# A long convolution and MLP on one core: the second half's two spectral products summed on VectorE before one step back, in a new hand-written order

## The chip, the cores and the metric

The kernel runs on one core of one Trainium2 chip. The metric is the device time of one execution in microseconds; the time before is the median of three runs. A profiled execution of the same program gives the trace; its span, from the first to the last instruction, is a little shorter than its device time.

The core has five engines with queues of their own, which run in the order in which instructions stand in them: TensorE (PE in the profile; its weight loads are listed as PEld), VectorE (DVE), ScalarE (ACT), GpSimd (POOL) and SyncE (SP, which here only starts DMA transfers). An instruction that waits holds up all that stands behind it in its queue.

## The reference

With S = 2048 rows, D = 512 channels and F = 1792:

```
kv = shift_conv4(k, shift_k) * v                                  # [S, D], four taps along S
y  = irfft(rfft(pad(kv)) * rfft(pad(ssm_k)))[:S] + kv * ssm_D     # causal convolution over S, per channel
h  = x + layernorm(x) * y                                         # x = A_q
n  = layernorm(h)
g  = gelu(layernorm(n) @ w1);  g shifted along S by -1, +1, -2, +2 rows in four channel groups;  x1 = n + g @ w2
out = h + x1 + gelu(layernorm(x1) @ w3) @ w4                      # bf16 in and out
```

The convolution is the part that the change touches: its product is made between two spectra, channel by channel.

## The kernel before

**Halves.** The sequence is cut into two interleaved halves of eight row blocks each. Tasks carry the half as `s` (0 or 1). A signal named A0 or A1 is the gated input kv of a half, F0 or F1 a half of the filter. The circular convolution of the whole becomes small ones: half 0 of the output needs the product A0 x F0, half 1 needs A0 x F1 + A1 x F0.

**Transforms as matmuls.** Each signal goes forward in two steps of small matmuls against tables of sines that are built at the start: `S1` (line 389), copied out of PSUM by `E1`, exchanged between partitions by eight DMAs `X` (L405), then `S2` (L413), copied out by `E2`. For F1 the copy also adds and subtracts the spectrum of F0 (a fold, L425, VectorE). E1, E2 and EV below all go through one helper, so that their copies stand at L257 in the profile, on ScalarE or VectorE as the order says.

**Product and step back.** `conv(s, prods)` (L465 to L496) works in four passes `kl`. In each, for every pair of spectra, VectorE makes two products of 128 x 2048 bf16 elements (tasks `P`, L474): one with the filter spectrum as it lies (x = 0) and one with its real and imaginary planes exchanged (x = 1). Each product goes to two of the eight buffers of `r_p`. After each, TensorE takes a step back `I2` (L484) of 16 matmuls of 32 x 64 weights, which accumulates in the same four PSUM banks. The first half has one pair, so two products and two steps per pass; the second half has two pairs, so four products and four steps. `EV` copies the four banks out, `XI` (L495) exchanges partitions by DMA, and `I1` (L502) is the last transform, after which VectorE forms `H` (L616): h with its row sum.

**The MLP around it.** For each pair of row blocks of a half: statistics of h, a normalised copy `hb` (L655 on GpSimd or VectorE, L653 on ScalarE), its transposes (by TensorE and a copy, or by DMA through DRAM), `W` (L699) and its gelu `U`, the mixing over rows `X2` (L722), its residual sum `S` (L725, VectorE) with a row statistic `SS`, a second normalised copy `lb`, transposes again (`LX`, with the copy `EX`), `M` (L777), seven steps of eight matmuls per pair, with gelus `G` (L781, ScalarE), and `O` (L790) per block, 14 matmuls against w4. `R` (L729) and `Z` (L792) are VectorE's last sums for a block, and `OUT` stores it. The MLP of the first half lies between the passes of the second half's convolution. `Q` (L506) are the row statistics of the query input, per block, and `QV`, `QP`, `QN`, `Y` make its normalised form; `dg` (L299 on GpSimd, L307 on VectorE) builds the diagonal matrices of the four taps, which the shift (`K`, L442) uses as weights; `KV` (L450) is the gating.

**What sets the order.** Tasks are declared with `add(name, engines, function, ...)`. The order in which their instructions are issued is written out in the string `ORDER` at the head of the file: each word is a task's number, the engine that takes it (P, V, A, G or S) and the PSUM banks or buffers that it takes. So the string fixes each engine's queue, the engine of each task that has a choice, and the place of every DMA on SP's queue. The numbers in braces in `add` are the costs and `port` a mark with which the string was once planned; they do nothing in the program. The waits between engines follow from the data and buffers that instructions share.

Of the kernel before, what the change touches and what calls it, by code (L numbers as in the profile page):

```python
# [9 lines left out]
P = 128  # L10
S = 2048
D = 512
# [3 lines left out]
NB = 8  # L16
XW = 258
KW = NB * 129 + 8

BF16 = mybir.dt.bfloat16  # L20
F32 = mybir.dt.float32
# [10 lines left out]
004S 029P0 000S 002S 003S 005S 008S 031V 037V 001S 030P 063P23 006S 055P45 009S 057P67 064V 007S 056A 038G 065P01 010S 058A 019S 059P45 033V 045G  # L32
061P23 060A 087P60 039G 036V 062A 095P71 046V 042V 066A 093P4 032G 043V 047A 074S 101P5 044A 034G 015S 094V 051P23 022S 088V 053P01 035G 023S 052A
040V 072S 089P4 024S 054A 049G 091P6 021S 090V 073S 041A 097P2 096V 050G 070S 092V 099P3 048A 069S 102V 068S 107P01 098V 109P67 017S 100V 108A 103P45
067S 110V 111P23 018S 104A 115P01 071S 113P67 112A 323V 105P45 324V 116A 211P20 106V 114A 117P01 212V 119S 118A 084P4567 326V 085A 081P2301 123S 329V
086V 120S 083A 215P4 020S 082A 330V 124S 078P0167 327V 125S 217P5 080A 216V 121S 079A 075P2367 012S 218V 011S 325V 076A 127P4501 016S 319V 328V 122S
077A 219P21 129V 126S 331G 128A 013S 220V 130P6701 139V01 132A 141V23 131A 133P4501 332G 134A 140P23670 147V45 142P 135A 333G 149V67 143A 337G0
148P45011 155V01 150P 343G1 144A 145S 221P2 340G2 157V23 152A 146S 334G3 014S 151A 136P6701 222V 137V 138A 156P23452 153S 158P 154S 163V45 225P0 159A
223P1 160A 165V67 161S 164P67230 162S 226V 166P 224V 175P45 167A 168V 213P0 176A 169S 183P67 214V 170S 185P23 184A 187P45 315S 186V 177P01 188A 189P67
178V 179P23 190A 181P45 180V 171P67 028S 182A 172P01 338V 192S 231P45 196S 335V 339A 349G0 173P23 316S 344V 336A 346G3 193S 341V 235P67 232A 355G1  # L40
195S 347V 174P10 236A 352G2 191S 350V 237P45 198S 358G 342A 356V 202P6723 197S 348A 353V 194S 345A 359G 204V 239P01 238A 371G 203V 241P23 240A 227P45
242A 229P01 372G 360V 228V 230A 199P6723 247S 361G0 373V 233P45 351A 364G1 200V 362P00 234A 374G2 365P1 384V 366A 377G3 208P6745 245S 363V 354A 375P11
243S 201V 385G 367P0 376A 244S 357A 378P1 386V 246S 369P2 379A 390V0 318S 209V 397G 387A1 382P3 248S 370A 250S 388P12 210V 368A 398G 391P6 249S 380P7
383A 389A 027S 392V 399G 251P2345 263V01 381A 393P0 253A 026S 400G3 265V23 395P1 025S 252A 317S 403V2 205P6745 396A 267V45 401P23 394A 404P3 502P1
402A 206V 405A 506P0 503V 408P2 507V 504A 406P3 269V67 508A 409A 264P67011 558V 407A 266P 207V 268P 559G 270P 560G 498P2 271A 272V 561G1 510P3 564G0
499V 274S 494P4 501V 273S 562P50 511V 565P6 514P7 563A 495V 566A 411V 254P0123 496A 567P50 515V 256A 275V01 569P4 568A 577P6 277V23 570A 257P2345 578A
412V 573P7 259A 255V 571P6 258A 279V45 579P4 572A 574A 281V67 575P5 580A 516A 276P01232 414V 500A 278P 513V 280P 576A 615G 512V 282P 581P6 505V 283A
616G 517V 284A 617G 413V 621G3 287V01 618A2 619P71 587G 622P4 582V 260P0123 620V 583S 584P5 623V 588G 262A 289V23 589G 291V45 591A1 590G0 293V67
624P40 593S 261V 636P6 592S 625A 634P7 416V 509V 288P23010 635A 594S2 290P 299V01 292P 285S 294P 301V23 628P4 296A 632P7 303V45 629A 298S 637A 626P0
286S 633A 305V67 630P1 295A 410V 627A 297S 300P67231 417V 631A 302P 415V 304P 306P 418V 641P4 307A 419G 308A 309S 310S 420V 421V0 427G3 638P0 424G1  # L50
430V2 585V 642V 497V 311P16 639V 312P72 640S 422V 643S 313P35 425V 423A 433G0 428V 314P40 426A 431V 439A3 595P10 445G 442V1 432A 603P2 436V2 429A 437V
597P6 596A 434V 446G 605P7 598A 438A 447V 599P1 448V2 435A 451G3 322V 458V 607P5 600A 470V 459G 449P33 452P6 601P1 450V 453A 471G 460V 604A 440V 454P6
602A 472G 441V 461A2 456P3 443V 474G1 462A3 444V 473G0 608A 476S 606A 612P2 482V 475S 457A 463S 483G 464S 609P1 484V 477S0 485A1 486G0 455A 487S 321V
488S 465S1 518P0 522P3 489S2 480P4 523V 478P5 519V 524A 468P3 520A 481A 466P7 644V 521V 645G 490P6 467A 525V 646G 469A 492P0 610V 320G 479A 647V2
534P3 491A 648V3 649S 493A 650S 542P4 535V 554P5 537V 536A 538P3 651S3 555V 546P7 543V 556A 586S 545V 526P1 544A 611S 539V 530P6 547V 540A 550P3 527V
# [38 lines left out]
def body(ctx, tc, fx, kt, q, v, sd, w1, w2, w3, w4, out):  # L94
# [200 lines left out]
    def dg(c):  # L295
        def f(e, sl):
            if e == GP:
                tap = r_k[:, c * KW + NB * 129:(c + 1) * KW].rearrange("p (j x) -> p j x", x=2)[:, :, 1:2]
                pool.affine_select(out=diag[:, c], in_=tap.to_broadcast([P, 4, P]), compare_op=OP.is_equal, fill=0.0, base=0,  # L299
                                   pattern=[[0, 4], [-1, P]], channel_multiplier=1)  # L300
                return
# [542 lines left out]
```

## Time and profile before

| | us |
|---|---|
| runs | 215.84, 214.04, 215.55 |
| median | 215.55 |
| profiled execution | 213.26 |
| its span | 211.6 |

The granted TensorE clock was 1.000 in the profiled execution. Its busiest groups on TensorE are the MLP's `M` and `O`; on VectorE the products, 24 in all; on ScalarE the copies out of PSUM and the gelus. DMA moved 32.86 MB, most of it in the first 80 us.

How to read the lines that follow: in the table of groups a line has the source line, engine, operation, what it writes and reads, the shape and count, then total busy us and the mean ns of one, then the engine's idle time just before them and what ended it. In a timeline a line has start, length, engine, source line, operation, count, and in brackets the idle time before it and its releaser. The chain of waits follows the work that ended last back from the end. In the slices, each digit is the busy share in tenths of a fortieth of the span.

### The profile page before, as it was taken

What the parts mean: (1) busy time and instruction counts of PE and PEld (TensorE: products, weight loads), DVE (VectorE), ACT (ScalarE), POOL (GpSimd) and SP (SyncE); (2) the same over time, 40 slices, a digit from 0 to 9 for tenths busy, and PEclk for the clock granted to TensorE, in tenths of its full rate; (3) what the DMA queues carried; (4) which work ended last, traced back from release to release, by engine and by line L of the source; (5) the groups of instructions that cost most, each with busy time, mean ns of one, the idle gap of its engine ahead of it and who ended that gap; (6) DMA issues with size and microseconds to landing.
All of it is one profiled execution on the core that took longest, in us unless ns stands there. A gap on an engine that the chain in (4) does not pass through costs nothing.

```text
span 211.6 us, 5040 instructions
## 1 busy us (share of the span) xinstructions
PE 195.7 (93%) x1964; PEld 116.2 (55%) x1980; DVE 144.8 (68%) x302; ACT 125.5 (59%) x206; POOL 80.1 (38%) x177
## 2 busy tenths in 40 slices
PE   6899769898889999979999999989999999999992
PEld 5454323442248546636744884645848888645450
DVE  6998999999999999999868971559972000112031
ACT  3979989787999658943751883364623565301010
POOL 7850059804888140287044683212765000000000
PEclk9999999999999999999999999999999999999999
DMA  6999895976948995000693008533146440010011
GB/s 173 313 403 397 321 325 222 256 205 237 371 169 294 332 435 147 0 28 13 89 232 92 27 22 181 98 69 82 42 107 154 102 74 0 3 50 34 16 50 50
DMA packets 30809, 32.86 MB, mean 155 GB/s; under 512 B 20545, under 2 KB 22594, under 8 KB 30530
## 3 DMA queue, kind: packets, MB, share of 16 engines
q1 hardware_dynamic: 30786, 32.55, 50.8%
q8 instruction: 15, 0.25, 0.5%
q14 instruction: 8, 0.07, 0.1%
HBM read 13.14 MB, written 4.46 MB: 83 GB/s over the span
## 4 chain that ended last, share of the span: by engine, by line
PE 59%; DVE 13%; ACT 12%; DMA 6%; issue 3%; POOL 3%; SPq 3%; DVEq 0%; ACTq 0%; POOLq 0%
PE ps L777 21%; PE ps L790 18%; ACT r_a L257 5%; PE ps L722 5%; PE ps L699 5%; PE ps L484 3%; DVE r_v L616 3%; DMA r_dg<-dhb 2%; DMA r_a<-r_a 2%; PE ps L502 2%; PE ps L413 2%; DMA r_k<-in_kt_dram 2%; DVE r_f L425 2%; DVE r_dg L307 1%; DVE r_p L474 1%
## 5 line engine op out<-in xcount | busy, mean ns | idle before, releaser
L777 PEld LDWEIGHTS <-r_k 128*128 128x128 bf16 x448 | 43.5, 98 | 7.7 <-issue 1.2
L792 DVE TENSOR_TENSOR r_v<-ps,r_v 128x512 bf16<-128x512 f32 x16 | 10.7, 686 | 42.4 <-PE ps L790 42.4
L474 DVE TENSOR_TENSOR r_p<-r_a,r_f 128x2048 bf16<-128x2048 bf16 x24 | 28.7, 1240 | 1.0 <-PE ps L484 0.6
L777 PE MATMUL ps<-r_dg,r_k 128*128 128x256 bf16 x224 | 25.6, 273 | 0.1
L257 ACT CAST r_a<-ps 128x1024 bf16<-128x1024 f32 x23 | 22.2, 1026 | 3.0 <-PE ps L413 2.8
L781 ACT ACTIVATE r_f<-ps 128x512 bf16<-128x512 f32 x14 | 7.8, 599 | 20.6 <-PE ps L777 20.6
L613 POOL TENSOR_SCALAR z_t<-r_q,qrs,qnm 128x512 f32<-128x512 bf16 x11 | 13.0, 1188 | 12.6 <-DVE r_v L616 12.0
L442 PE MATMUL ps<-r_dg,r_k 128*128 128x256 bf16 (+3 forms) x108 | 15.2, 284 | 1.6 <-ACT r_f L257 0.8
L257 ACT CAST r_vs<-ps 128x1024 bf16<-128x1024 f32 x14 | 13.7, 1032 | 4.9 <-PE ps L484 4.9
L725 DVE SCALAR_TENSOR_TENSOR r_q<-r_v,hrr,ps 128x512 bf16<-128x512 bf16 x16 | 11.4, 742 | 5.9 <-PE ps L722 3.7
L781 ACT ACTIVATE r_a<-ps 128x512 bf16<-128x512 f32 x14 | 7.8, 606 | 12.2 <-PE ps L777 12.2
L257 ACT CAST r_f<-ps 128x1024 bf16<-128x1024 f32 x14 | 13.2, 1023 | 3.0 <-PE ps L389 2.8
L442 PEld LDWEIGHTS <-r_k 128*128 128x128 bf16 x112 | 9.5, 98 | 9.5 <-issue 4.8
L484 PE MATMUL ps<-r_p,ttab 32*64 32x512 bf16 x384 | 13.3, 379 | 1.0 <-DVE r_p L474 0.8
L699 PEld LDWEIGHTS <-r_fx 128*128 128x128 bf16 x128 | 12.3, 98 | 3.2 <-DMA r_dg<-dhb 0.6
L600 ACT ACTIVATE junk<-r_v 128x512 bf16<-128x512 bf16 x14 | 8.9, 635 | 7.3 <-DVE r_v L616 7.1
L777 PE MATMUL ps<-xtx,r_k 128*128 128x256 bf16 x112 | 13.0, 273 | 0.0
L600 ACT ACTIVATE junk<-r_q 128x512 bf16<-128x512 bf16 x12 | 7.6, 630 | 9.2 <-DVE r_q L725 9.1
L777 PE MATMUL ps<-xty,r_k 128*128 128x256 bf16 x112 | 12.7, 272 | 0.0
L790 PE MATMUL ps<-w4s,r_f 128*128 128x512 bf16 x54 | 12.5, 379 | 0.1
L748 POOL TENSOR_TENSOR xrr<-xrr,mhalf 128x2 f32<-128x2 f32 x8 | 7.2, 900 | 14.2 <-DVE xrr L745 13.8
L389 PEld LDWEIGHTS <-f 128*32 128x32 bf16 x256 | 6.1, 95 | 11.3 <-issue 7.5
(183 smaller groups left out, 374.7 us busy)
## 6 DMA issues: line engine op xcount, KB each, us to landing
r_z<-r_vs SPq DMA_DIRECT2D x16, 256.0 KB, 3.9
r_k<-in_kt_dram SPq DMA_DIRECT2D x8, 260.0 KB, 4.6
r_v<-in_v_dram SPq DMA_DIRECT2D x4, 512.0 KB, 7.3
r_f<-r_f SPq DMA_DIRECT2D x8, 256.0 KB, 5.2
r_q<-in_q_dram SPq DMA_DIRECT2D x8, 256.0 KB, 5.7
r_a<-r_a SPq DMA_DIRECT2D x8, 256.0 KB, 4.2
r_f<-r_a SPq DMA_DIRECT2D x8, 256.0 KB, 4.2
r_a<-r_z SPq DMA_DIRECT2D x8, 256.0 KB, 4.1
```

The lines of the kernel that those rows point to most:

```text
L257: (act.copy if e in "AM" else on[e].tensor_copy)(o, i)
L442: nc.tensor.matmul(o[:, (d + j0) * P:(d + j1 + 1) * P], lhsT=kT[s][c][:, bb, x:x + P], rhs=diag[:, c, j0:j1 + 1, :].rearrange("p j x -> p ...
L474: on[e].tensor_tensor(out=prs[:, sl[0]:sl[0] + 2, :, :], in0=sp[a][:, kl, :, :, :], in1=gv, op=MUL)
L484: nc.tensor.matmul(ps[64 * t:64 * t + 64, bk[h], :], lhsT=ttab[32 * h:32 * h + 32, 2 * kl + t, 2 if x else xx, :], rhs=prs[32 * h:32 * h + ...
L600: act.activation(junk[:], x, ACT.Square, accum_out=sq[:, i, 1:2])
L613: on[e].tensor_scalar(out=z_t[:, sl[0], :], in0=qs, scalar1=qrs[:, i:i + 1], scalar2=qnm[:, i:i + 1], op0=MUL, op1=ADD)
L699: nc.tensor.matmul(ps[:, sl[0], j * 256:(j + 1) * 256], lhsT=w1s[:, k, m * P:(m + 1) * P], rhs=xt[:, k, :], start=(k == 0), stop=(k == DC ...
L725: vec.scalar_tensor_tensor(out=q_sb[:, s, b, :], in0=h_sb[s][:, b, :], scalar=hrr[:, 4 * s + b // 2, 0, b % 2:b % 2 + 1], in1=ps[:, got((" ...
L777: nc.tensor.matmul(ps[:, sl[0], j * 256:(j + 1) * 256], lhsT=w3s[:, k, fc * P:(fc + 1) * P], rhs=xt[:, k, :], start=(k == 0), stop=(k == D ...
L781: act.activation(gb[:, 2 * fp:2 * fp + 2, :], ps[:, got(("M", s, p, fp))[0], :].rearrange("p (j x) -> p j x", j=2), ACT.Gelu_apprx_tanh)
L790: nc.tensor.matmul(ps[:, sl[0], :], lhsT=gb[:, fc, (b % 2) * P:(b % 2 + 1) * P], rhs=w4s[:, fc, :], start=(fc == 0), stop=(fc == FC - 1))
L792: add(("Z", s, b), {V: 0.61}, lambda e, sl, b=b: vec.tensor_tensor(out=h_sb[s][:, b, :], in0=ps[:, got(("O", s, b))[0], :], in1=h_sb[s][:, ...
```

## The change

**The sum of products.** In `conv`, if there is more than one pair (the second half), VectorE adds the second pair's product to the first's in place (`PA`), and the step back is made on the sum alone: two steps `I2` per pass in both halves. The steps' weights don't depend on the pair, so the sum is the same but for a rounding to bf16. The second product's buffers come free with the addition. The rule that each product must follow the one declared before it is dropped.

```
-                    before = last_p[-1:]
...
-                    add(("P", s, kl, i, x), {V: 1.15}, f, [("E2", y, kl, t) for y in (a, g) for t in range(2)] + ["f2"] + before, take=[("pr", -1)], port="VG")
-                    last_p.append(("P", s, kl, i, x))
-                    first, last = (i, x) == (0, 0), (i, x) == (len(prods) - 1, 1)
...
+                    add(("P", s, kl, i, x), {V: 1.15}, f, [("E2", y, kl, t) for y in (a, g) for t in range(2)] + ["f2", "tt"], take=[("pr", -1)], port="VG")
+                    first, last, y = x == 0, x == 1, ("P", s, kl, 0, x)
+                    if i < len(prods) - 1:
+                        continue
+                    if i:
+                        def f(e, sl, x=x, kl=kl):
+                            pa, pb = (prs[:, got(("P", s, kl, j, x))[0]:got(("P", s, kl, j, x))[0] + 2, :, :] for j in range(2))
+                            vec.tensor_tensor(out=pa, in0=pa, in1=pb, op=ADD)
+                        add(("PA", s, kl, x), {V: 1.135}, f, [y, ("P", s, kl, i, x)], drop=[(("P", s, kl, i, x), 0)], port="VG")
+                        y = ("PA", s, kl, x)
```

**Row statistics of the query input.** For blocks 4 to 7 of the second half they are made by ScalarE, as a sum and a sum of squares, in place of one pass on VectorE; the variance step takes three more short instructions for them.

```
+        if s == 0 or b < 4:
+            return lambda e, sl: vec.bn_stats(qst[:, 8 * s + b, :], q_sb[:, s, b, :])
+
+        def f(e, sl):
+            act.activation(junk[:], q_sb[:, s, b, :], ACT.Identity, accum_out=qst[:, 8 * s + b, 0:1])
+            act.activation(junk[:], q_sb[:, s, b, :], ACT.Square, accum_out=qst[:, 8 * s + b, 1:2])
+        return f
```

**Diagonals.** `dg` can be made by GpSimd only; before, VectorE made two of the four (four instructions each) and GpSimd two.

**The order.** `ORDER` is a new string throughout: places in all queues, the engine of many tasks that have a choice, and banks. What the steps of the prediction speak of:

- VectorE, up to its last spectral pass: besides the eight additions it takes the first half's `QV` and `QN`, two `Y` and some short passes; it gives up both `dg`, five `Q` of the second half (four to ScalarE; those of blocks 1 to 3 now follow, and that of block 0 does as before), four `R` (they follow later), and on balance three copies out of PSUM (`E1`, `EV`) to ScalarE. The `EX` copies of blocks 2 and 3 are VectorE's now, those of blocks 0 and 1 ScalarE's.
- ScalarE: the four `Q`, the copies `E2` of A1 in pass 1 and 3, `EV` of passes that VectorE copied in part.
- GpSimd: four `dg`; `dr` and `f2v` (table and input preparation at the start) go to VectorE.
- TensorE: one `M` step of the first half's pair 2 stands ahead of the last pass `I2`; the second half's `I1` steps are interleaved with `M` steps; the first `M` of the second half's pair 1 precede `O` of blocks 6 and 7 of the first half.
- SP: `Lw3` and `Lw4`, the loads of w3 and w4 of 1.8 MB each, precede more of the second half's exchanges `X`; some input loads come later.

More of the change, by code (lines that the diff above doesn't have):

```diff
@@ L36 @@
[L36 to L39, printed above, removed]
@@ L296, in f @@
         def f(e, sl):
[L297 to L301, printed above, removed]
[L302 to L307 removed]
+            tap = r_k[:, c * KW + NB * 129:(c + 1) * KW].rearrange("p (j x) -> p j x", x=2)[:, :, 1:2]
+            pool.affine_select(out=diag[:, c], in_=tap.to_broadcast([P, 4, P]), compare_op=OP.is_equal, fill=0.0, base=0,
+                               pattern=[[0, 4], [-1, P]], channel_multiplier=1)
         return f
     for c in range(DC):
[L310 removed]
+        add(("dg", c), {GP: 0.65}, dg(c), [("Lk", 0, c)], port="VG")
     sv = small("sv", 8, F32)
@@ L461, in kvsrc @@
         return lambda b: kvs[:, got(("K", 2 * s + b // 4, 0), "kv")[0], b % 4, :]
-    last_p = []
     def conv(s, prods):
```

85 lines of the change are left out of this document (43 added, 42 removed).

## The prediction

> **What bounds the kernel now.** I read the page first (engine totals, the span in slices), then the windows over the stages that it suggests, then the chain of waits and single engines' timelines where stages meet.
>
> ```profile
> span 211.6 us, 5040 instructions
> ...
> PE 195.7 (93%) x1964; PEld 116.2 (55%) x1980; DVE 144.8 (68%) x302; ACT 125.5 (59%) x206; POOL 80.1 (38%) x177
> ...
> DVE  6998999999999999999868971559972000112031
> ```
>
> TensorE is busy for 93% of the span, but VectorE's row of slices holds nines almost to the middle and little in the last quarter. The kernel has two regimes, and the windows separate them (after the length: PE, PEld, DVE, ACT, POOL, then the granted clock, 1.00 throughout):
>
> ```profile
> 49.60:69.20 19.60, 18.00 (x225) 8.98 (x226) 19.18 (x48) 18.39 (x35) 16.16 (x32) 1.00 0.74 269
> 69.20:109.70 40.50, 38.91 (x529) 23.61 (x519) 37.95 (x62) 26.94 (x45) 13.97 (x24) 1.00 0.52 154
> ...
> 113.90:207.90 94.00, 92.71 (x626) 61.06 (x632) 38.63 (x107) 39.28 (x81) 23.54 (x44) 1.00 0.28 65
> ```
>
> From 113.9 on TensorE has work for 92.7 of 94.0 us and the others for two fifths: there the end is TensorE's alone. From 49.6 to 109.7 TensorE and VectorE are both nearly full; in the second stretch only ScalarE has room, 40.50 - 26.94 = 13.6 us. The chain of waits shows how the regimes meet:
>
> ```profile
> 102.26 3.60 PE ps L777 x32
> 105.86 1.87 PE ps L484 x64
> 107.73 0.16 issue
> 107.89 5.99 PE ps L790 x27
> 113.88 0.04 issue
> 113.92 3.61 PE ps L502 x16
> ...
> 207.82 0.69 DVE r_v L792
> ```
>
> The last pass of the second half's step back (L484, 64 matmuls) ends at 107.73, two output blocks of the MLP (L790) fill 6.0 us, and the second half's last transform (L502) starts at 113.92. In those 6 us the result is copied out by ScalarE and carried over by DMA:
>
> ```profile
> 101.04 4.63 DVE L474 TENSOR_TENSOR r_p<-r_a,r_f 128x2048 bf16<-128x2048 bf16 x4 [0.63 <-PE ps L484]
> 105.58 1.87 DVE L506 BATCH_NORM_STATS2 qst<-r_q 128x6 f32<-128x512 bf16 x3
> ...
> 107.78 1.93 ACT L257 CAST r_vs<-ps 128x1024 bf16<-128x1024 f32 x2 [1.03 <-PE ps L484]
> ```
>
> VectorE's last product ends at 105.6, just as TensorE reaches that pass; ScalarE's copies end at 109.7; the transform starts 4.2 later and TensorE has hardly idled. Three engines arrive level.
>
> **What the change costs, part by part.**
>
> *Matmuls taken away.* Each of the second half's four passes loses two of its four steps. A pass takes 1.87, a step so 0.47, and 8 steps are 3.7 us of TensorE, all ahead of 107.7. It is a gain only if TensorE then doesn't wait for what feeds the transform.
>
> *Additions put on VectorE, and what leaves it.*
>
> ```profile
> L474 DVE TENSOR_TENSOR r_p<-r_a,r_f 128x2048 bf16<-128x2048 bf16 x24 | 28.7, 1240 | 1.0 <-PE ps L484 0.6
> L729 DVE SCALAR_TENSOR_TENSOR r_v<-r_q,hnm,r_v 128x512 bf16<-128x512 bf16 x16 | 11.5, 740 | 0.1
> ...
> L257 DVE CAST r_a<-ps 128x1024 bf16<-128x1024 f32 x9 | 10.8, 1214 | 0.4 <-PE ps L389 0.3
> ...
> L425 DVE TENSOR_TENSOR r_f<-ps,r_f 128x512 bf16<-128x512 f32 x16 | 10.1, 679 | 0.0
> L307 DVE TENSOR_SCALAR r_dg<-ident,r_k 128x128 bf16<-128x128 bf16 x8 | 3.1, 466 | 0.5 <-DMA r_k<-in_kt_dram 0.5
> ...
> L613 DVE TENSOR_SCALAR z_t<-r_q,qrs,qnm 128x512 f32<-128x512 bf16 x4 | 2.0, 541 | 0.0
> ...
> L655 DVE TENSOR_SCALAR nbx<-r_q,xrr,xnm 128x512 bf16<-128x512 bf16 x3 | 1.1, 407 | 0.0
> ```
>
> No row shows an addition. The nearest is the product, which moves the same three tiles: 4.63/4 = 1.16 apiece in a run, 1.24 on the mean. Four block scalings (0.41 each) move as many elements and take longer, so no row gives a lower bound under 1.16. I take 1.16: eight are 9.3 us (up to 9.9).
>
> Comparing the two queues up to VectorE's last spectral pass: five row statistics leave (1.87/3 = 0.62 apart, 3.1), four residual sums move behind (0.74, 3.0), three copies out of PSUM go to ScalarE on balance (1.21, 3.6), both diagonal builds go to GpSimd (3.1): 12.8 off. On come the 9.3, two query passes (0.54, 1.1), the first half's variance in nine steps of a few elements, which I estimate at a third of a block scaling each (1.2), and on balance two short passes (0.41, 0.8): 12.4. Net -0.4: the additions are paid for.
>
> Two waits are new. VectorE, not ScalarE, now copies the transposes of the first half's blocks 2 and 3. Between the residual sum that they start from and that copy, its queue holds an addition, four folds and three sums, 1.2 + 4 x 0.68 + 3 x 0.74 = 6.1. The way from sum to copy, in the trace:
>
> ```profile
> 72.71 0.74 DVE L725 SCALAR_TENSOR_TENSOR r_q<-r_v,hrr,ps 128x512 bf16<-128x512 bf16 x1
> ...
> 78.62 1.07 ACT L257 COPY r_dg<-ps 128x512 bf16<-128x512 bf16 x2 [1.89 <-PE ps L670]
> ...
> 88.53 0.76 POOL L589 TENSOR_SCALAR xsq<-xsq 128x4 f32<-128x4 f32 x1 [10.52 <-ACT junk L600]
> ...
> 90.21 1.03 POOL L748 TENSOR_TENSOR xrr<-xrr,mhalf 128x2 f32<-128x2 f32 x1
> ```
>
> From 73.45 to 78.62 it takes 5.2; its variance moves from VectorE to GpSimd, where one takes 1.7 (88.53 to 90.21), so the way becomes 6 to 7: a wait of 0 to 1.0, and all of VectorE's second half is queued behind it. Likewise VectorE now takes a scale factor behind GpSimd's power (1.03): 0 to 1.0. I take 1.0 and 0.8. The 0.63 in brackets above, a wait for a product's buffer, goes, since additions free buffers early. The last spectral pass then ends at 105.6 - 0.4 - 0.6 + 1.8 = 106.4 (105.0 to 107.5), its step 0.5 later: 106.9, 0.8 earlier than now.
>
> *What goes onto ScalarE.*
>
> ```profile
> 72.82 0.63 ACT L600 ACTIVATE junk<-r_q 128x512 bf16<-128x512 bf16 x1 [1.61 <-DVE r_q L725]
> 73.36 0.19 ACT L600 ACTIVATION_READ_ACCUMULATOR junk<-r_q 128x1 f32 x1
> 73.57 0.63 ACT L600 ACTIVATE junk<-r_q 128x512 bf16<-128x512 bf16 x1
> ...
> 98.39 0.81 ACT L653 ACTIVATE r_k<-r_q,xnm,xrr 128x512 bf16<-128x512 bf16 x1 [2.63 <-POOL xnm L756]
> ...
> 103.28 1.57 ACT L781 ACTIVATE r_v<-ps 128x512 bf16<-128x512 f32 x3
> ```
>
> Four of the row statistics, two passes each, 0.75 apart: 6.0. Three copies of 0.97: 2.9. Two gelus (0.52): 1.0. These 9.9 us take ScalarE from 26.9 to 36.8 us in the stretch of 40.5. It enters it 0.8 later (one more block scaling ahead). Two waits can't be filled: one behind GpSimd's power (2.63 here; I take 2.1) and the one for the last pass (1.03). Its last copy ends at 69.2 + 0.8 + 36.8 + 2.1 + 1.0 = 109.9, 0.2 later than now, and the transform starts at 114.1. That is where the matmuls' gain goes: TensorE, 3.7 lighter, waits. Bounds: 108.5 if its waits fall together; 113 if only half of the 13.6 us can be used (9.9 - 6.8 = 3.1 spill over).
>
> *GpSimd* gains two diagonal builds and is to run between products. What a meeting costs:
>
> ```profile
> 59.85 1.53 POOL L655 TENSOR_SCALAR nbx<-r_v,hrr,hnm 128x512 bf16<-128x512 bf16 x2
> ...
> 66.81 2.84 POOL L655 TENSOR_SCALAR nbx<-r_v,hrr,hnm 128x512 bf16<-128x512 bf16 x1
> ...
> L474 DVE TENSOR_TENSOR r_p<-r_a,r_f x24: 1205/1219/1708, 30.4 to 104.4; 128x2048 bf16<-128x2048 bf16 x24
> ```
>
> A scaling of 0.77 took 2.84 beside two products, 1.0 more for each; the products kept to 1.2 (one of 24 reached 1.71). I charge VectorE nothing. [...]
>
> *Start and loads.* A freer VectorE starts the first products earlier, but all copies behind the first half's last pass now go to ScalarE; I take 0, with 1.5 either way. On SP's queue the load of w3 now stands ahead of five of the second half's eight exchanges (three before) and that of w4 ahead of three (none before):
>
> ```profile
> r_a<-r_z SPq DMA_DIRECT2D x8, 256.0 KB, 4.1
> ...
> w4s<-in_w_dram SPq DMA_DIRECT2D x1, 1792.0 KB, 14.4
> ...
> xtx<-dlb SPq DMA_TRANSPOSE x2, 3.4
> ```
>
> An exchange lands in 4.1, the large load in 14.4. What queues behind it lands later, hidden while TensorE's own queue is later still; I take 0, up to +2.
>
> *Behind the transform.* One MLP step (3.60/4 = 0.9) moves ahead of it, so TensorE has 94.0 - 0.9 = 93.1. The second half's first MLP steps now precede two output blocks, so 6.0 us of cover for their transposes (3.4 by DMA, after writes) is gone; six mixing and six MLP steps, some 10.6 us, remain. I take 0, up to +1.5. VectorE's 0.4 more work between its last pass and the first gated sum is hidden by the transform.
>
> **The sum.** Transform +0.2, rest -0.9: -0.7. The profiled execution took 213.26 (span 211.6 and 1.7 around it) and becomes 212.6; the runs' median, 215.55, lies 2.3 above it, which I carry over: 214.85. This case's own range is -2.3 to +1.5: 213.2 to 217.1.
>
> **Rivals.** *The whole gain comes through.* ScalarE's additions fit into its idle time, VectorE arrives at 105, and TensorE is 3.7 shorter: 211.9. For it: -0.4 on VectorE. Against: the engines arrive level already, and ScalarE is to be 91% full.
>
> *Slower: ScalarE becomes the bound of the middle.* It drains in order, so a copy that a product needs stands behind statistics and scalings that wait for others. With half of its idle time usable, 3.1 us spill into all later steps: 218.7. It decides once less than some 9 of the 13.6 us serve. For it: much of that idle time stands in front of instructions that wait for VectorE or GpSimd (1.61 and 2.63 above). Against: its queue was rearranged as well.
>
> *The port.* GpSimd's scalings meet products on the way to two transposes that TensorE needs, 1.0 to 1.2 each: 2.4 less the 0.7, 217.3. For it: eight passes more to meet. Against: fewer scalings on GpSimd.
>
> That the change doesn't do what it says is excluded: the changed program has 128 matmuls less and eight VectorE passes more.
>
> **How the numbers follow.** The runs spread over nearly 1%, so within 1% (2.2 us) is about what can't be told from no change. Forecast 0.34 (within 0.28, faster 0.04, slower 0.02); whole gain 0.29 (faster); ScalarE 0.25 (slower); port 0.12 (slower 0.08, within 0.04). So faster 0.33, within 0.32, slower 0.35. The range runs from 211.0, the whole gain with 0.9 of the start's 1.5, to 219.8, the ScalarE case with 1.1 of the tail's 1.5.
>
> **What would show it.** Right: VectorE's last addition near 106, each of 1.16; ScalarE busy for about 37 us in the forty before its last copy; the transform at about 114 with TensorE idle some 3 us more ahead of it. Wrong: TensorE as full as now and the transform at 111 (whole gain); copies of the second half's spectra long after their matmuls, with VectorE idle in front of products (ScalarE); scalings of 2 us and more in front of transposes, or additions of 2 us (port); a gap on TensorE in front of the second half's MLP steps (tail).

## The result, and the profile after

| | changed kernel | kernel before, run beside it |
|---|---|---|
| median of 16 runs | 217.51 us | 214.38 us |
| range | 215.26 to 219.21 | 213.13 to 215.84 |
| profiled execution, its span | 216.18, 214.0 | 213.26, 211.6 |

The ratio is 1.0102, 95% interval 1.0072 to 1.0132: one per cent slower. Medians here and below are over all runs; a ratio leaves out the runs that the comparison took for disturbed, here four of the sixteen of the changed kernel, so it can lie below the quotient of the medians (1.0146).

The page of the changed kernel, to be held against the first lines of the prediction:

```profile
span 214.0 us, 4799 instructions
...
PE 193.8 (91%) x1836; PEld 114.6 (54%) x1852; DVE 153.6 (72%) x321; ACT 131.7 (62%) x217; POOL 65.2 (30%) x160
...
DVE  6799999998999999789996987648994260002121
...
PEclk9999999999958999999999999999999999999998
```

TensorE has 1.9 us less to do and the span is 2.4 us longer. The clock row, all nines before, has a 5 and an 8. Where the time went is told by the stretch from the first half's last transform to the second half's. First the window of the kernel before (length; busy PE, PEld, DVE, ACT, POOL; granted clock), then that of the changed kernel, with two pieces of it:

```profile
48.50:113.90 65.40, 62.14 (x762) 34.80 (x769) 60.89 (x117) 45.90 (x80) 32.60 (x57) 1.00 0.61 191
```

```profile
48.40:115.88 67.48, 61.16 (x642) 33.93 (x649) 61.32 (x114) 55.38 (x103) 30.50 (x58) 0.95 0.56 182
54.00:57.20 3.20, 0.73 (x20) 0.15 (x16) 3.02 (x10) 3.17 (x9) 2.41 (x7) 1.00 1.02 389
57.20:65.00 7.80, 7.34 (x90) 2.62 (x91) 7.56 (x16) 7.28 (x13) 6.96 (x15) 0.60 0.31 121
```

The start is level (48.5 and 48.4). TensorE is busy for 1.0 us less and idle for 6.3 us, where it was 3.3; that is the 2.1 us by which the second transform is late. Its busy time has fallen so little because 57 to 65 us ran at a clock of 0.60 (a matmul of S2, L405, took 614 ns on the mean between 58.7 and 65.5, and 381 to 382 after 66) and because an `M` step has moved into the stretch. TensorE's timeline of the changed kernel names the large waits (in brackets), the last two of them behind the second transform:

```profile
48.39 1.90 PE L496 MATMUL ps<-r_z,f 128*128 128x512 bf16 x7 [1.41 <-DMA r_z<-r_vs]
...
57.17 0.63 PE L405 MATMUL ps<-r_f,ftab 64*32 64x512 bf16 x16 [2.22 <-DMA r_f<-r_a]
...
84.23 0.62 PE L405 MATMUL ps<-r_a,ftab 64*32 64x512 bf16 x16 [2.34 <-DMA r_a<-r_z]
...
142.18 6.50 PE L728 MATMUL ps<-r_fx,r_f 128*128 128x512 bf16 x28 [0.75 <-ACT r_f L709]
...
177.97 4.54 PE L783 MATMUL ps<-xtx,r_k 128*128 128x256 bf16 x40 [0.62 <-DMA xtx<-dlb]
```

The two of over 2 us are for exchanges: F1's in front of the first S2 step, A1's in front of its second. In front of its own first S2 step of F1 and second of A1 the kernel before waits 0.29 us and not at all:

```profile
54.26 0.62 PE L413 MATMUL ps<-r_f,ftab 64*32 64x512 bf16 x16 [0.29 <-DMA r_f<-r_a]
...
79.60 0.63 PE L413 MATMUL ps<-r_a,ftab 64*32 64x512 bf16 x16
```

SP's timeline of the changed kernel shows where the exchanges stood, F1's first and then A1's, and the chain of waits how long the last one took:

```profile
47.78 3.90 SPq L397 DMA_DIRECT2D r_f<-r_a  x4
51.78 0.53 SPq L266 DMA_DIRECT2D r_fx<-in_w_dram  x1
52.41 0.40 SPq L266 DMA_DIRECT2D r_q<-in_q_dram  x1
52.86 2.98 SPq L397 DMA_DIRECT2D r_f<-r_a  x4
```

```profile
66.22 0.43 SPq L266 DMA_DIRECT2D r_k<-in_w_dram  x1
66.70 1.30 SPq L397 DMA_DIRECT2D r_a<-r_z  x2
68.04 0.81 SPq L266 DMA_DIRECT2D w4s<-in_w_dram  x1
68.89 0.72 SPq L397 DMA_DIRECT2D r_a<-r_z  x1
69.70 0.53 SPq L266 DMA_DIRECT2D r_q<-in_q_dram  x1
70.28 1.57 SPq L397 DMA_DIRECT2D r_a<-r_z  x2
```

```profile
70.28 13.82 DMA r_a<-r_z
84.10 0.14 issue
84.23 0.62 PE ps L405 x16
```

An exchange of 256 KB of A1, issued at 70.28 behind the loads of w3 and w4 (3.6 MB), took 13.8 us; TensorE stood still for it. From issue to landing A1's three exchanges ahead of both loads took 2.3 to 3.7 us, the two behind the load of w3 9.8 each, and the three behind both 13.4 to 13.9. In the kernel before the median was 4.1: the five ahead of the load of w3 took 2.6 to 4.1, the three behind it 9.0 to 9.1.

The two waits are not of one kind. From issue to landing the changed kernel's exchanges take, on the median,

```profile
r_f<-r_a SPq DMA_DIRECT2D x8, 256.0 KB, 4.2
r_a<-r_z SPq DMA_DIRECT2D x8, 256.0 KB, 9.8
```

A1's are slow, behind the loads. F1's are as fast as before, but in the new order TensorE takes pass 0 of S2 first, and an exchange of that pass stands fifth of the eight, behind the loads of w1 and of a block of q: it is issued at 52.86, 4.3 us before TensorE can start.

VectorE's timeline shows the same lateness at second hand, and GpSimd's what else is there:

```profile
86.89 1.23 DVE L462 TENSOR_TENSOR r_p<-r_a,r_f 128x2048 bf16<-128x2048 bf16 x1 [0.33 <-ACT r_a L257]
88.96 0.16 DVE L591 SCALAR_TENSOR_TENSOR xmv<-xsq,xmv 128x2 f32<-128x2 f32 x1 [0.78 <-ACT junk L606]
95.46 1.56 DVE L462 TENSOR_TENSOR r_p<-r_a,r_f 128x2048 bf16<-128x2048 bf16 x1 [0.83 <-ACT junk L505]
97.05 1.68 DVE L470 TENSOR_TENSOR r_p<-r_p 128x2048 bf16<-128x2048 bf16 x1
...
107.56 1.23 DVE L470 TENSOR_TENSOR r_p<-r_p 128x2048 bf16<-128x2048 bf16 x1
```

```profile
60.13 2.48 POOL L661 TENSOR_SCALAR nbx<-r_v,hrr,hnm 128x512 bf16<-128x512 bf16 x2
...
95.18 2.48 POOL L661 TENSOR_SCALAR r_k<-r_q,xrr,xnm 128x512 bf16<-128x512 bf16 x2
```

VectorE waits 0.33 and 0.78 us behind ScalarE, which copies what TensorE makes late. The 0.83 is put down to ScalarE's row statistics, but these are done at 94.6; the buffers that this product writes come free with TensorE's step back, which starts at 94.69. An addition is 1.2 us, but 1.68 beside two GpSimd scalings. The last addition ends at 108.8, where the forecast had 106.4.

### The profile page after: what moved, and what is told of

It reads as the page before. It is cut to its first block, busy times and chain, and to the rows that moved or that the text cites. A ratio compares the mean times of both kernels' runs of the same rounds, so it can differ in the third digit from the quotient of the medians.

```text
span 214.0 us, 4799 instructions
## 1 busy us (share of the span) xinstructions
PE 193.8 (91%) x1836; PEld 114.6 (54%) x1852; DVE 153.6 (72%) x321; ACT 131.7 (62%) x217; POOL 65.2 (30%) x160
## 4 chain that ended last, share of the span: by engine, by line
PE 62%; DMA 16%; DVE 8%; ACT 5%; SPq 4%; issue 3%; POOL 1%; ACTq 0%; DVEq 0%
PE ps L796 22%; PE ps L783 20%; DMA r_a<-r_z 6%; PE ps L705 4%; PE ps L728 4%; PE ps L496 3%; PE ps L405 2%; DMA r_q<-in_fx_dram 2%; DMA r_z<-r_vs 2%; DMA r_k<-in_kt_dram 2%; SPq L397 2%; PE ps L479 2%; ACT r_a L257 2%; DVE r_kv L442 2%; SPq L266 2%
## 5 line engine op out<-in xcount | busy, mean ns | idle before, releaser
L798 DVE TENSOR_TENSOR r_v<-ps,r_v 128x512 bf16<-128x512 f32 x16 | 10.8, 689 | 36.5 <-PE ps L796 36.3
L783 PE MATMUL ps<-r_dg,r_k 128*128 128x256 bf16 x280 | 32.1, 273 | 0.0
L462 DVE TENSOR_TENSOR r_p<-r_a,r_f 128x2048 bf16<-128x2048 bf16 x24 | 29.3, 1251 | 1.4 <-ACT junk L505 0.8
L257 ACT CAST r_a<-ps 128x1024 bf16<-128x1024 f32 x26 | 24.7, 1027 | 5.8 <-PE ps L405 3.0
L257 ACT CAST r_vs<-ps 128x1024 bf16<-128x1024 f32 x16 | 15.4, 1013 | 2.1 <-PE ps L479 1.5
L535 POOL TENSOR_TENSOR qrs<-qsd,mhalf 128x8 f32<-128x8 f32 x2 | 3.3, 1654 | 43.6 <-DMA r_z<-r_vs 28.5
L783 PE MATMUL ps<-xtx,r_k 128*128 128x256 bf16 x112 | 13.4, 273 | 0.6 <-DMA xtx<-dlb 0.6
L257 ACT CAST r_f<-ps 128x1024 bf16<-128x1024 f32 x12 | 11.6, 1027 | 3.0 <-PE ps L381 2.9
L787 ACT ACTIVATE r_kv<-ps 128x512 bf16<-128x512 f32 x14 | 7.9, 590 | 8.0 <-PE ps L783 8.0
L796 PE MATMUL ps<-w4s,r_v 128*128 128x512 bf16 x53 | 12.3, 379 | 0.2
L796 PE MATMUL ps<-w4s,r_kv 128*128 128x512 bf16 x54 | 12.3, 379 | 0.1
L796 PE MATMUL ps<-w4s,r_a 128*128 128x512 bf16 x55 | 12.2, 379 | 0.1
```

Source lines behind the costliest of these rows:

```text
L257: (act.copy if e in "AM" else on[e].tensor_copy)(o, i)
L462: on[e].tensor_tensor(out=prs[:, sl[0]:sl[0] + 2, :, :], in0=sp[a][:, kl, :, :, :], in1=gv, op=MUL)
L783: nc.tensor.matmul(ps[:, sl[0], j * 256:(j + 1) * 256], lhsT=w3s[:, k, fc * P:(fc + 1) * P], rhs=xt[:, k, :], start=(k == 0), stop=(k == D ...
L787: act.activation(gb[:, 2 * fp:2 * fp + 2, :], ps[:, got(("M", s, p, fp))[0], :].rearrange("p (j x) -> p j x", j=2), ACT.Gelu_apprx_tanh)
L796: nc.tensor.matmul(ps[:, sl[0], :], lhsT=gb[:, fc, (b % 2) * P:(b % 2 + 1) * P], rhs=w4s[:, fc, :], start=(fc == 0), stop=(fc == FC - 1))
L798: add(("Z", s, b), {V: 0.61}, lambda e, sl, b=b: vec.tensor_tensor(out=h_sb[s][:, b, :], in0=ps[:, got(("O", s, b))[0], :], in1=h_sb[s][:, ...
```

## The experiments

Medians and ratios are each against the kernel before, run on the same chip beside it. "X,F1 1,0" is the exchange of F1 for the half 1 of its blocks and pass 0.

**Exchanges in order of use.** Three kernels, each with SP's queue alone changed. The first (F1):

```
-    Lw2   X,F1 0,1  1,3  1,2  0,0   Lw1  Lq,1,1   X,F1 1,0  0,2  0,3  1,1
+    Lw2   X,F1 0,0  0,3  1,0  1,3  0,1  1,1  0,2  1,2   Lw1  Lq,1,1
```

> The changed kernel with one stretch of SP's queue put in another order: the eight exchanges X,F1 in the order in which TensorE's steps S2,F1 use them, and the loads of w1 and of a block of q behind them. Theory that the lost time is the late exchanges: TensorE's idle 2.22 us in front of the first S2,F1 step falls under 0.4. VectorE reaches its first fold at 57.98 with 0.15 us of idle time, so nothing is gained there at once; what is gained is the clock: 1.00 in every run, where the changed kernel has 0.98 to 1.00, and a median near the low end of its runs, 215.4 us. Rival, that the loss is VectorE's own extra work in the second half (56.21 us busy between its first H and its last addition, against 54.44): the idle time goes, the time stays at 217.5.

The second (A1):

```
-    X,A1 0,3  0,0  1,0   Lq,1,0  Lq,1,2  Lw3   X,A1 1,3  0,2   Lw4   X,A1 1,1   Lq,1,3   X,A1 0,1  1,2
+    X,A1 0,0  0,1  0,2  0,3   Lq,1,2   X,A1 1,0  1,1  1,2  1,3   Lq,1,0  Lw3  Lw4  Lq,1,3
```

> The changed kernel with another stretch of SP's queue reordered: the eight exchanges X,A1 in the order of use, the loads of w3 and w4 and of two blocks of q behind them. Late-exchange theory: TensorE's 2.34 us of idle time in front of S2,A1,1 (84.23) go, so do VectorE's waits of 0.33, 0.78 and 0.83 behind it, its last addition ends at about 106.9 instead of 108.8, the second half's transform starts at about 114.0 instead of 115.9, the time is 215.6. Rival (VectorE's own work, and ScalarE's row statistics in front of its copies): the waits of 0.78 and 0.83, which name ScalarE, stay, the last addition ends at 108.2 or later, and the time is 217 or more.

The third has both.

> Both reorderings together. Late-exchange theory: the two gains add, 2.1 and 1.9 us, 213.5, within 0.5% of the kernel before and perhaps below it. Rival (VectorE's work): 217 and more.

Measured: 216.88 (ratio 1.0085, 1.0044 to 1.0126), 217.31 (1.0125, 1.0082 to 1.0168) and 217.56 (1.0144, 1.0091 to 1.0198). None gains. In the third, no step of A1 waits for an exchange any more, and VectorE's three waits are gone (others of 0.79 and 0.97 us have come), yet TensorE idles 5.8 us between the transforms (69.39 less 63.60; the profile is of the longest of the six runs, 219.83):

```profile
50.86:120.25 69.39, 63.60 (x648) 34.98 (x649) 61.98 (x114) 55.73 (x102) 36.18 (x58) 0.93 0.53 175
```

So late exchanges are not the whole cause, or something stands behind them.

**The additions alone, in the old order.** The kernel before with `conv` as in the change, an addition on VectorE behind the second product of each pair, and the second product's buffers given out in turn.

> The kernel before, its order kept, with the additions alone: each of the eight sums stands on VectorE right behind the second of its two products, and TensorE's two later steps of each pass are gone; row statistics, copies and scalings stay on the engines where they were. If VectorE is the bound of the middle: eight additions of 1.22 us come on, the 0.63 us wait for a buffer goes, its last spectral pass ends at 105.6 + 9.1 = 114.7 and the time is 8 to 9 us over the kernel before, about 223. If TensorE's matmuls are the bound there and VectorE has room: 3.7 us less, about 211.

Measured 225.0 (ratio 1.0487, 1.0425 to 1.0549). TensorE's timeline has VectorE as the releaser in front of nearly every step back; these are the last pass:

```profile
113.74 0.64 PE L487 MATMUL ps<-r_p,ttab 32*64 32x512 bf16 x16 [1.26 <-DVE r_p L478]
116.14 0.64 PE L487 MATMUL ps<-r_p,ttab 32*64 32x512 bf16 x16 [1.76 <-DVE r_p L478]
```

In the old order VectorE is the bound, and the change of `conv` costs 10.7 us by the medians. The new order wins 7.5 of them back (225.0 to 217.5).

**Is it the clock?** Matmuls that do nothing were put where TensorE waits, and the same with both exchanges in order:

```
+    def fill(bank, n):
+        for _ in range(n):
+            nc.tensor.matmul(ps[:, bank, :], lhsT=ident[:], rhs=ftab[:].rearrange("p a r x -> p (a r x)")[:, 0:512], start=True, stop=True)
...
+            fill(sl[0], 6 if (s, b) == (0, 0) else 0)
...
+            fill(sl[0], 9 if sig == "F1" and kl == 0 else 0)
```

> The changed kernel with matmuls that only keep TensorE busy: six (identity against a constant table, 0.22 us each) in front of the first half's transform and nine in front of the step S2,F1,0, written to a bank that the next step overwrites. Nothing else is moved. Clock theory (the idle time of 1.41 and 2.22 us there makes the granted clock fall to 0.50 to 0.69 between 58 and 66 us, and that is what spreads the runs from 215.26 to 219.2): the clock stays at 1.00 in 40 to 76 us, and the median falls to about 215.5 with a narrow spread. Rival (TensorE has slack there, VectorE sets the end of the second half's step back whatever the clock): 217.5 as without the filler, VectorE's last addition at 108.8 as before.

> Both reorderings of SP's queue together with the filler. The reordered queue alone gave no gain, but its profile had two clock drops, and in it VectorE's three waits of the eighties and nineties were gone. If the clock hid the gain: clock 1.00 and 213.5 to 214.5. If VectorE's work is the bound, the waits that go return elsewhere: 215.5 and more, no better than the filler alone.

Measured 217.32 (1.0133, 1.0081 to 1.0185) and 216.89 (1.0120, 1.0067 to 1.0173). The windows of the first (a run of 219.36, its longest) show that the spell at 58 to 66 us is gone; another stands behind the wait for A1's exchange, which the filler doesn't cover:

```profile
58.00:66.00 8.00, 6.12 (x98) 2.73 (x97) 7.74 (x18) 7.61 (x15) 7.11 (x15) 1.00 0.28 107
84.00:92.00 8.00, 7.04 (x61) 5.34 (x62) 5.57 (x10) 5.27 (x10) 4.19 (x5) 0.79 0.02 5
```

Over the runs the mean granted clock rose from a median of 0.984 to 0.998, and the time stayed. So the clock is not the cause by itself. That the spells cost nothing isn't shown: over the sixteen runs of the changed kernel time and clock go together (215.26 and 215.71 us in the two runs with 0.999 or more, a median of 219.1 in the six with 0.982 or less). Longer waits would do that too, and the filler's own matmuls may use up part of what it saves. The second kernel's trace shows what stands behind the exchanges:

```profile
63.55 1.04 PE L682 MATMUL ps<-ident,nbx 128*128 128x128 bf16 x8 [1.33 <-POOL nbx L667]
...
96.62 0.62 PE L682 MATMUL ps<-ident,nbx 128*128 128x128 bf16 x8 [1.85 <-POOL nbx L667]
```

TensorE now waits in front of two transposes for GpSimd's scalings, those which run beside VectorE's products and folds. (With the filler alone the first of these waits is there already, 1.34 us.)

**Is it VectorE's work?** The additions cut to 8 of 2048 columns:

```
-                            vec.tensor_tensor(out=pa, in0=pa, in1=pb, op=ADD)
+                            vec.tensor_tensor(out=pa[:, 0, 0, 0:8], in0=pa[:, 0, 0, 0:8], in1=pb[:, 0, 0, 0:8], op=ADD)
```

> The changed kernel with each addition cut to 8 of its 2048 columns; it leaves out the sum of the two spectral products. It tells what the additions cost in the new order. VectorE as the bound of the middle: 8 x 1.1 = 8.8 us of VectorE go, its last spectral pass ends near 100 and TensorE, whose pass then waits for nothing, takes over; the time falls by 3.5 us or more, to 214 or less. If the exchanges, ScalarE's copies or the clock set the middle: less than 1 us, 216.5 or more.

Measured 218.09 (1.0144, 1.0085 to 1.0203): no gain at all. VectorE is 9 us lighter and waits instead:

```profile
L462 DVE TENSOR_TENSOR r_p<-r_a,r_f 128x2048 bf16<-128x2048 bf16 x16 | 19.9, 1261 | 6.1 <-ACT junk L505 3.0 <-PE ps L479 2.2 <-ACT r_a L257 0.7
L470 DVE TENSOR_TENSOR r_p<-r_p 128x8 bf16<-128x8 bf16 x8 | 1.3, 159 | 0.2
```

The idle time in front of its products has grown to 6.1 us. VectorE is not the bound of the changed order. This is where the forecast's path by VectorE (its last pass at 106.4, the step back at 106.9) fell.

**GpSimd's scalings.** Cut to 8 of 512 columns for the first half, with the filler (and `nbx` set to zero once, early):

```
+            w = slice(0, 8) if e == GP and s == 0 else slice(0, D)
-            on[e].tensor_scalar(out=o, in0=i, scalar1=sc, scalar2=bi, op0=MUL, op1=ADD)
+            on[e].tensor_scalar(out=o[:, w], in0=i[:, w], scalar1=sc, scalar2=bi, op0=MUL, op1=ADD)
```

> The changed kernel with the filler, and with the first half's block scalings on GpSimd cut to 8 of 512 columns (seven or so that meet VectorE's products); it leaves out the rest of those blocks, whose norms the MLP then reads as zeros. Port theory: products and additions, which take 1.25 and 1.28 us on the mean with single ones of 1.4 to 1.7, all come to 1.21 to 1.23; VectorE's last addition is 1.2 us earlier than with the filler alone, and so is the end. Rival (GpSimd alone pays for a meeting, as forecast): the means stay at 1.25 and the time with them.

Measured 216.96 (1.0103, 1.0051 to 1.0155), not to be told from the filler alone. The two groups of products and additions, first with the filler alone, then with the scalings cut:

```profile
L463 DVE TENSOR_TENSOR r_p<-r_a,r_f 128x2048 bf16<-128x2048 bf16 x16 | 20.1, 1273 | 1.1 <-ACT junk L511 0.9
L471 DVE TENSOR_TENSOR r_p<-r_p 128x2048 bf16<-128x2048 bf16 x8 | 10.2, 1279 | 0.2
```

```profile
L464 DVE TENSOR_TENSOR r_p<-r_a,r_f 128x2048 bf16<-128x2048 bf16 x16 | 19.3, 1218 | 2.1 <-ACT r_a L257 1.0 <-ACT junk L512 0.8
L472 DVE TENSOR_TENSOR r_p<-r_p 128x2048 bf16<-128x2048 bf16 x8 | 9.8, 1222 | 0.2
```

The meetings do lengthen VectorE's passes, by 16 x 0.055 + 8 x 0.057 = 1.3 us; it gets that back, and TensorE then waits 3.16 us for A1's exchange. Each cause stands in front of the other.

**Both causes at once.** First with the scalings cut, then as a whole computation. The two moves beside the exchanges are

```
 VectorE   E2,F1,0  [- P,1,0,0,1]  E2,F1,3  hn,0,2  [+ P,1,0,0,1]  E2,F1,1  ...
 VectorE   ...  xn,0,0  [+ lb,0,0]  lb,0,1  P,1,2,0,0  ...
 GpSimd    ...  r1,0,0  [- lb,0,0]  lb,0,5  lb,0,4
```

> The changed kernel with both reorderings of SP's queue, the filler, and the first half's GpSimd block scalings cut to 8 of 512 columns (it leaves out the rest of those blocks). Theory now: TensorE is the path from the first half's transform on; it has 3.7 us of matmuls less there, but idles 6.3 us (the kernel before: 3.3) for several things that are late at about the same time (exchanges, GpSimd's scalings for two transposes), and idle time of about 2 us within a few us is followed by 3.4 us or more at half clock. Taking one away let the next appear. With both away: TensorE's idle time between the two transforms falls to about 3 us, the clock is 1.00, the second transform starts 3 to 4 us earlier, at about 112.5, and the time is 213.5 to 214. Rival (VectorE's work sets the end): 216 to 217, the idle time of TensorE stays and moves in front of the last passes of the step back.

> The whole computation, changed kernel with four moves in its order: the eight exchanges of each of F1 and A1 ahead of the loads, the first product of the second half on VectorE put behind the folds and the scale factor that follow it, and one block scaling in front of a transpose given from GpSimd to VectorE. By the TensorE theory two of the five waits for GpSimd or exchanges (2.22, 2.34, and 1.33 and 1.85 with the exchanges mended) shrink to less than 0.7 each, the clock falls at most once, and the time is 214.0 to 215.5. By VectorE's: 217.

> The same four moves with a short filler: five matmuls in front of the first half's transform, four in front of S2,F1,0. TensorE theory: as the run without filler or up to 1 us less, since no clock spell is left in 45 to 70 us: 213.5 to 215. VectorE's: 217.

Measured 214.78 (1.0023, 0.9999 to 1.0047), 214.85 (1.0007, 0.9973 to 1.0040) and 214.54 (0.9987, 0.9958 to 1.0016). The loss is gone in all three. The first differs from the exchanges with filler (1.0120) by the scalings alone. In the second, the whole computation, GpSimd's two scalings take 1.53 where they took 2.48, which speaks for the meetings with VectorE rather than GpSimd's own work as what made them late (no run parts the two), and TensorE idles 3.5 us between the transforms:

```profile
59.89 1.53 POOL L661 TENSOR_SCALAR nbx<-r_v,hrr,hnm 128x512 bf16<-128x512 bf16 x2
```

```profile
48.15:113.81 65.66, 62.20 (x649) 34.63 (x649) 61.19 (x115) 55.12 (x102) 30.10 (x57) 0.95 0.58 188
```

It did so with a clock spell of about 7 us inside the stretch (0.50 from 60 to 66), in a run of 213.62, and the three shortest of its twelve runs (213.26 to 213.62) all have a clock of 0.984: there the spell is not the price. The third, without such a spell, has its last addition at 106.45 and the second transform at 113.14; the forecast had 106.4 and 114.1.

```profile
48.54:113.14 64.60, 60.42 (x654) 34.17 (x653) 60.75 (x115) 54.83 (x103) 31.12 (x57) 1.00 0.60 190
```

**The two moves without the exchanges.**

> The changed kernel with the two moves on VectorE and GpSimd alone (the product behind the folds, the block scaling from GpSimd to VectorE), SP's queue as in the changed kernel. If only both groups together help, because each removes a gate behind which the other stands: 217 to 217.5, TensorE still idles 2 us and more in front of S2,F1,0 and S2,A1,1. If the moves were the whole cure: 214.5 to 215.

Measured 216.17 (1.0100, 1.0065 to 1.0136), TensorE idle for 2.75 and 2.12 us in front of the two steps (in the profile of its longest run, 219.00). So neither group helps alone and both together do. Which of the two moves does more, and whether F1's or A1's exchanges do, was not tried.

**The new queue order in the kernel before.** SP's queue alone, with X,A1 among the loads as the changed kernel has it:

```
-    X,A1 1,0  0,2  0,0  0,1  0,3   Lw3   X,A1 1,1  1,3  1,2   Lq,1,2  Lq,1,1  Lq,1,0  Lw4
+    X,A1 0,3  0,0  1,0   Lq,1,0  Lq,1,2  Lw3   X,A1 1,3  0,2   Lw4   X,A1 1,1   Lq,1,1   X,A1 0,1  1,2
```

> The kernel before, nothing changed but SP's queue, where the exchanges X,A1 stand among the loads of w3, w4 and q in the changed kernel's order. If late exchanges cost time by themselves: TensorE, which reaches S2,A1,1 at 79.6 us, waits there 2 to 4 us for an exchange that lands at 82 to 84, and the time rises by 2 to 4 us, to 216.5 to 218.5. If TensorE has slack there because VectorE arrives last: under 1 us more, 214.4 to 215.4.

Measured 219.54 (1.0246, 1.0211 to 1.0282), 5.2 us more than the kernel before, beyond what either theory gave. TensorE's wait, and the transfer that it waits for in the chain:

```profile
84.97 1.05 PE L413 MATMUL ps<-r_a,ftab 64*32 64x512 bf16 x16 [2.94 <-DMA r_a<-r_z]
```

```profile
71.11 13.72 DMA r_a<-r_z
```

Much the same time, in a kernel without additions. The place of the loads costs time by itself. How much of the 5.2 us is theirs is less clear: from transform to transform the profiled run takes 68.76 us against 65.40, 3.4 more, of which the wait is 2.9, and the clock fell to 0.50 in 86 to 88. Another 2.4 us lie ahead of the first transform (50.88 against 48.50), where the two kernels' queues are the same; why was not followed up.

**The additions cut, in the mended order.**

> The mended order with the short filler and each addition cut to 8 of 2048 columns; it leaves out the sum of the two spectral products. In the changed order the same cut gained nothing. If VectorE, busy without a gap from 57 to 106 us in the mended order, is now the bound: its last spectral pass ends 3 us and more earlier and the time falls by 1.5 us or more, to 213 or less. If TensorE's own matmuls and waits are the bound here too: 214 to 215.

Measured 214.62 (1.0016, 0.9986 to 1.0046). From transform to transform it takes 64.45 us, and 64.60 with the additions. VectorE has hardly a gap in the mended order and still isn't the bound: in the new order, mended or not, the eight additions cost nothing that can be measured.

**ScalarE's row statistics cut** to 8 of 512 columns, in the changed kernel:

```
-            act.activation(junk[:], q_sb[:, s, b, :], ACT.Identity, accum_out=qst[:, 8 * s + b, 0:1])
-            act.activation(junk[:], q_sb[:, s, b, :], ACT.Square, accum_out=qst[:, 8 * s + b, 1:2])
+            act.activation(junk[:, 0:8], q_sb[:, s, b, 0:8], ACT.Identity, accum_out=qst[:, 8 * s + b, 0:1])
+            act.activation(junk[:, 0:8], q_sb[:, s, b, 0:8], ACT.Square, accum_out=qst[:, 8 * s + b, 1:2])
```

> The changed kernel with the four row statistics that went to ScalarE cut to 8 of 512 columns each; it leaves out the rest of those four rows' sums. About 4 of the 6 us that they cost ScalarE between 69 and 112 us go. Rival of the prediction, ScalarE as the bound of the middle: its copies come earlier, the transform starts 2 us and more earlier, 215.5 or less. TensorE's waits for exchanges as the cause: no gain, 217 to 218, with 2 us of idle time in front of S2,A1,1 as before.

Measured 216.58 (1.0053, 1.0009 to 1.0098). The interval overlaps that of the changed kernel: a gain of between nothing and 1% (the difference of the ratios, 0.5%, with both intervals put together). In its trace the last addition ends at 111.0 and TensorE still waits 2.92 us for F1's exchange. That profile is of a run of 217.18, 3.6 above the shortest. VectorE's wait of 0.83 in front of the product stays, though the statistics to which it was put down are cut. ScalarE may have a part in the loss; that its statistics need not cost anything is shown by the mended order, which keeps them whole and loses nothing.

**The tail.** The mended order with the short filler and three moves behind the second transform (after the engine, the tasks of its queue; digits are PSUM banks):

```
 SP        LT,1,5  LT,1,4  [+ TE,1,4]  LT,1,7  LT,1,6  [- TE,1,4]  TE,1,6
 TensorE   X2,1,2: bank 1 -> 5    X2,1,5: bank 5 -> 1    (M,0,3,4 M,0,3,6 M,0,3,5 follow)
 TensorE   M,1,3,2  [+ M,1,0,4  M,1,3,5]  M,1,2,0  ...  O,1,5  [- M,1,0,4  M,1,3,5]  O,1,7
```

> The whole computation: the mended order with the short filler, and three more moves behind the second transform (a transpose in front of two writes on SP's queue, the bank of two mixing steps swapped so that none waits for the last gelu, two MLP steps put in front of those that wait for a transpose). The three waits there are 1.23, 0.75 and 0.32 us in the mended kernel. If they are on the path: 1.5 to 2 us less than the mended order, 212.5 to 213.5, faster than both kernels. If something else takes their place: 214.5.

Measured 218.07 (1.0148, 1.0095 to 1.0200). The miss is told by one line of TensorE's timeline:

```profile
138.67 1.92 PE L711 MATMUL ps<-xtx,r_fx 128*128 128x256 bf16 x16 [2.78 <-DMA xtx<-dhb]
```

By the order of SP's queue the moved transpose has to wait for its own writes, and the two writes behind it wait along; that is read from the order, not from a trace of SP in this run (in the kernel before SP waits up to 2.8 us in front of a transpose for its writes). Shown is that TensorE waits 2.78 us for the transpose of the two. It is the mistake of the change once more, made by hand.

## Why the prediction was wrong

**The step that failed is the one on loads**, in "Start and loads": what queues behind a large load lands later, "hidden while TensorE's own queue is later still; I take 0, up to +2". TensorE's queue was not later: it waited 2.34 us for A1's exchange, which took 13.8 us. F1's exchanges, for which it waited 2.22, the prediction doesn't name at all. In the kernel before, the A1 part of that order costs 5.2 us by the medians and 3.4 from transform to transform, both over the bound taken. The prediction had both rows at hand, 4.1 us for an exchange and 14.4 for the load, and the trace of before has 9.0 to 9.1 for the exchanges behind the load of w3; it compared none of them with the time at which TensorE takes up S2, which stands in the trace of before (79.6 for the second A1 step).

**The port** was a rival at 0.12, with its place named rightly: GpSimd's scalings on the way to two transposes. It is the second half of the cause, seen once the gaps ahead of it were closed (1.33 and 1.85 us), and taking it away brought 1.0120 to 1.0023. The runs don't rank the halves: with either one left, the loss stays (1.0144 and 1.0100). "I charge VectorE nothing" was wrong as well: 1.3 us, by the groups above (1273 to 1218 ns and 1279 to 1222). On GpSimd's side the cost of a meeting was as the rival had it, 1.0 to 1.2: a scaling of 0.77 us took 1.84 beside one product in the kernel before (91.80) and 1.97 in the changed kernel (93.22). That a port is what makes both longer no run shows. For the end, though, TensorE's waits for the transposes counted, not VectorE's 1.3 us.

**Start**: 48.39 for the first transform against 48.50: no change, as taken. **Matmuls taken away**: the steps' group between the transforms went from 7.7 to 4.5 us, near the 3.7 forecast. The stretch took in the moved M step (1.0) and, by my estimate, lost the other 1.2 to the clock of 0.60 (S2's matmuls of F1 alone went from 3.2 to 4.0 us), so that busy time fell by 1.0; idle time grew by 3.1.

**VectorE's ledger** was off by its place. Busy time from its first H to its last spectral pass was 54.5 before and 56.2 after, +1.7 where the text had -0.4: the diagonals' 3.1 us lie ahead of that stretch, where they moved the first H only from 49.66 to 49.10. That would make +2.7; the other 1.0 was not followed up. The two waits that were taken (1.0 and 0.8) did not come; three others did (0.33, 0.78, 0.83), which go with the exchanges. One of them is a wait for a product's buffer, of the kind that was to go. But this part rests on VectorE's arrival setting the last pass, and the two runs with the additions cut show that it doesn't.

**ScalarE**, which set the transform's 114.1 in the sum, was given 36.8 us for its forty and had 33.9; up to its last copy it had 36.3 in 42.9, so its work was sized well. That copy ended at 112.1, not 109.9, because the last pass came late; in the mended order with filler it ended at 109.3. The rival named for it, 218.7, lies near what was measured, and so does the port's 217.3; a time that fits is no evidence for its mechanism.

**Behind the transform**: -0.9 was taken, +0.5 measured (94.4 against 93.9), by the new waits of 0.75 and 0.62: 1.4 us, just inside the bound of 1.5.

**The sum**: the carried-over 2.3 us between profile and median was too much; over 16 runs it was 1.1. Without that error the forecast would have been 213.7 and the miss 3.8 us instead of 2.7. With both halves of the cause away, the ratios of 1.0007 and 0.9987 come near the 0.997 that was forecast (214.85 to 215.55); since VectorE's ledger and the part behind the transform were off too, that is partly luck.

Why the mended order gains nothing over the kernel before: between the transforms it is 0.8 us shorter at full clock (64.60 with 0.9 of filler in it, against 65.40). The span behind the start of the second transform went from 97.7 to 98.9 us in that run and 98.0 in the one without filler, though 0.9 us of matmuls had moved ahead. What was won ahead of it is spent there.

## What to carry to other kernels

When a change rewrites the order of a DMA queue, read for each transfer when its consumer will ask for it, and put what is asked for soon ahead of what is large: behind two loads of 1.8 MB an exchange took 13.4 to 13.9 us here, ahead of them 2.3 to 3.7. Work taken off an engine that is 93% busy is a gain only if what feeds it comes earlier too: before pricing the new work on other engines, list the waits of the engine that sets the end. Where undoing one suspected cause gains nothing, undo it together with the next before acquitting it: here each of two gates hid the other.

## What the runs showed of the hardware

- Half-clock spells followed some of TensorE's idle times and not others. In the changed kernel the wait of 2.22 us (in 3.2 us that held 0.73 us of work) was followed by a clock of 0.60 on the mean over the next 7.8 us, 0.50 from 59.0 to 65.5; the wait of 2.34 us for A1's exchange was followed by 1.00 throughout (84.23 to 94.70). So the "idle time of about 2 us" of one expectation is not enough by itself. In the kernel before with the new queue order the wait of 2.94 us was followed by 0.50 in 86 to 88. As an estimate from the means over windows of 2 us, this spell and the one from 86 us on in the changed kernel with the filler (0.50, then 0.65) lasted 3.4 us, those around 60 us in the changed kernel and in the mended order 6.8. What starts and ends a spell no run shows. In the mended order the spell stands in one of the three shortest runs; what the spells cost in the changed kernel stays open.
- All kernels with the changed order are alike ahead of the first half's transform but for a few filling matmuls and the first of F1's exchanges, yet in their profiles it starts between 48.15 and 50.86 us. A single profile can be 2 us off for that reason; stretches were compared from transform to transform.
